# Strassen block products in the last down-projection of a transformer block

## The chip, the cores and the metric

The kernel runs on one core of a Trainium2 chip. The core has engines that run side by side: TensorE multiplies matrices (the profile calls it PE, and its weight loads PEld), VectorE (DVE), ScalarE (ACT) and GpSimd (POOL) work element by element, and SyncE (SP) issues the DMAs. The metric is the device time of one execution in microseconds (us), as a median of several runs.

## The reference

```python
h = x + attention(layernorm(x), wq, wk, wv, wo, beta)     # 2048 tokens, 1024 wide
...
y = layernorm(h)
gate = y @ w1                  # w1, w3: 1024 x 3584
up = y @ w3
out = (silu(gate) * up) @ w2   # w2: 3584 x 1024, the down-projection
return h + out                 # 2048 x 1024, bfloat16
```

The attention works on four segments of 512 tokens with a memory carried between them. It comes first and the change does not touch it.

## The kernel before

The feed-forward part is split into two blocks of 1024 tokens. For each block, `hm[0]` to `hm[27]` hold silu(gate) * up transposed: 128 of the 3584 features on the partitions, the 1024 tokens along the row. `w2` holds all of the 3584 x 1024 weight on the chip, as 28 chunks of 128 rows.

The stages from the end of the attention on are these. `ffn_up(0, ch)` is the up-projection of the first block, in plain matmuls. `ffn_down(0, ...)` is its down-projection. `products7` is the up-projection of the second block, in 28 blocks of 28 matmuls, one for each `hm[n]`; it already takes 2x2 block products with 7 in place of 8 products, with fp16 sums of both operands: `T` holds sums of w1 and w3 columns (VectorE, three instructions a block, L1578), `S` sums of the tokens' tiles, and the products are put together by VectorE in `uu`, `ww` (L1603) and `cc` (L1613) and by GpSimd in `c22` (L1607, the profile calls it c). ScalarE copies partial products out of PSUM (L1600) and takes the silu (L1620, L734). `ffn_down(1, ...)` is the last stage, the down-projection of the second block.

`ffn_down` walks over eight tiles of 128 tokens. For each tile and each half of the 1024 output columns, a group of 28 matmuls (128 tokens x 128 features by 128 features x 512 columns) adds up in one PSUM bank; the groups take turns in banks 2, 3, 4 and 5. VectorE then multiplies by a scale and adds the tile's row of h (`hr`, three buffers, fetched by DMA from `h_scr`), writing `ob` (four buffers), and a DMA stores `ob`. The very last tile has its columns cut into 512, 256, 128 and 128, so that little is left after the last matmul. All matmuls are issued on one line, L763.

`weight_scale` finds power-of-two scales for w1 and w3 from sums of squares: ScalarE squares the weight tiles (L1407), VectorE reduces, one small matmul with a tile of ones adds over the partitions, and VectorE and GpSimd finish the scale. ScalarE multiplies the w1 and w3 tiles by it in `products7` (L734).

Every instruction of these last stages carries a plan time (`G.clock`, in us from the start of `ffn_down(0)`; `MM` = 0.2165 is the planned time of one matmul). Each engine, SP's DMA queue too, issues its instructions strictly in the order of the plan times, and each waits on semaphores for what it reads, and for what still reads or writes what it overwrites. In plan time `products7` begins at 97.0 and `ffn_down(1)` at 266.7. The first small matmul of `weight_scale` has the plan time 55.

Of the kernel before, what the change touches and what calls it, by code (L numbers as in the profile page):

```python
# [17 lines left out]
MM = 0.2165  # L18
# [577 lines left out]
class Kernel:  # L596
# [13 lines left out]
    def plan(self):  # L610
        g = self.g
        at = [16512]
# [49 lines left out]
        r6 = at[0]  # L662
# [17 lines left out]
        last = self.g.base[self.et[8].name][1]  # L680
# [10 lines left out]
        for i, off in enumerate((r2, r2 + 8192)):  # L691
# [28 lines left out]
        self.sq = buf("sq", [128, 32], F32, small + 256)  # L720
        self.sqb = buf("sqb", [128, 2], BF16, small + 384)
        self.sc = buf("sc", [128, 8], F32, small + 416)
# [681 lines left out]
    def squares(self, src, n, early=0):  # L1404

        out, to = self.sq[:, n:n + 1], self.junk2[early]
        return self.g.op("act", act_ns(2048) + 190, lambda e, gr: [e.activation(  # L1407
            to, src, AF.Square, accum_out=out)], reads=[src], writes=[to, out])

# [43 lines left out]
        gr.banks = banks  # L1453
        return gr

    def ffn_down(self, blk, at, inv=None):
        G = self.g
        for i in range(8):
# [5 lines left out]
            cols = [(0, 512), (512, 256), (768, 128), (896, 128)] if t == 15 else [(0, 512), (512, 512)]  # L1464
            for c0, n in cols:
                G.clock = start + 2 * 28 * MM * c0 / 1024
                gr = self.fixed((2, 3, 4, 5)[self.n_ob % 4])
                self.mms(gr, [(lambda gr, n=n: self.bank(gr, 0, n),
                               self.hm[fc][:, i * 128:(i + 1) * 128],
                               self.w2[fc // 4][:, fc % 4, c0:c0 + n],  # L1470
                               fc == 0, fc == 27, n) for fc in range(28)], 8, eager=True,
                         pause=None if t else at + 17.15 + c0 / 10240)
                ob = self.ob[self.n_ob % 4][:, 0:n]
                self.n_ob += 1
                hs = hr[:, c0:c0 + n]
                G.clock = start + 2 * 28 * MM * (c0 + n) / 1024 + (0.3 if t else 13.0)
                if inv is None:
                    G.op("dve", dve_ns(n), lambda e, gr, hs=hs, ob=ob, n=n: [e.tensor_tensor(
                        ob, hs, self.bank(gr, 0, n), op=ALU.add)], reads=[hs], writes=[ob], cls=1,
                        group=gr)  # L1480
                else:
                    G.op("dve", dve_ns(n), lambda e, gr, hs=hs, ob=ob, n=n: [
                        e.scalar_tensor_tensor(ob, self.bank(gr, 0, n), inv, hs, op0=ALU.mult,  # L1483
                                               op1=ALU.add)],
                        reads=[hs, inv], writes=[ob], cls=1, group=gr)
                G.clock += 0.8
                G.dma(self.out2d[t * 128:(t + 1) * 128, c0:c0 + n], ob, cls=1)
# [10 lines left out]
    def weight_scale(self, at):  # L1498

        G = self.g  # L1500
        one, sq, sqb, sc = self.ones[:, :], self.sq, self.sqb[:, :], self.sc
# [9 lines left out]
        G.clock = at + 42.0  # L1511
        n2, al, inv, tmp = (sc[:, 2 * i:2 * i + 2] for i in range(4))
        self.dve_op(lambda e: e.tensor_reduce(n2, sq[:, 0:28].rearrange(
            "p (c b) -> p b c", b=2), mybir.AxisListType.X, ALU.add), 200.0,
                    [sq[:, 0:28]], [n2])
        G.clock += 0.3
        self.dve_op(lambda e: e.tensor_copy(sqb, n2), 200.0, [n2], [sqb])
        G.clock = at + 55.0
# [3 lines left out]
        G.op("dve", 200.0, lambda e, gr: [e.tensor_scalar(n2, self.bank(gr, 0, 2), 1e-30, None,
                                                          op0=ALU.max)], writes=[n2], group=gr)
        G.clock += 0.5
        mh = self.mhalf[:, :].to_broadcast([128, 2])
        self.pool_op(lambda e: e.tensor_tensor(tmp, n2, mh, op=ALU.pow), 1, [n2, self.mhalf[:, :]], [tmp])
        G.clock += 1.0
        ti = tmp.bitcast(I32)
        self.dve_op(lambda e: e.tensor_single_scalar(ti, ti, 0x7F800000, op=ALU.bitwise_and), 200.0,
                    [tmp], [tmp])  # L1530
        G.clock += 0.2
        self.dve_op(lambda e: e.tensor_scalar(al, tmp, 4096.0, None, op0=ALU.mult), 200.0,  # L1532
                    [tmp], [al])
        G.clock += 0.2
        self.dve_op(lambda e: e.reciprocal(inv, al), 200.0, [al], [inv])
        return al, inv

    def token_sums(self, at):
# [9 lines left out]
            self.dve_op(lambda e, o=o, x=x, y=y, op=op: e.tensor_tensor(o, x, y, op=op),  # L1548
                        dve_ns(2048, 2), [x, y], [o])

    def products7(self, at, al, inv):

        G = self.g
        a, b = self.hnT[2], self.hnT[3]
# [2 lines left out]
        for n in range(28):  # L1557
# [39 lines left out]
            u, w, cc = self.uu[:, :], self.ww[:, :], self.cc  # L1597
            for gr, gr2, o, when in ((gb, gc, w, 1.1), (ga, gd, u, 2.85)):
                G.clock = t + when
                G.op("act", act_ns(512), lambda e, gr, o=o: [e.activation(  # L1600
                    o, self.bank(gr), AF.Copy)], writes=[o], group=gr)
                G.clock += 0.85
                G.op("dve", dve_ns(512), lambda e, gr, o=o: [e.tensor_tensor(  # L1603
                    o, self.bank(gr), o, op=ALU.add)], reads=[o], writes=[o], group=gr2)
            c22 = self.c22[:, :]
            G.clock = t + 4.4
            self.pool_op(lambda e: e.tensor_tensor(c22, u, w, op=ALU.add), 512, [u, w], [c22],  # L1607
# [5 lines left out]
            G.op("dve", dve_ns(1024), lambda e, gr, k=k: [e.tensor_tensor(  # L1613
                cc[:, :, :], self.ps[:, (k + 2) * 512:(k + 4) * 512].rearrange(
                    "p (a n) -> p a n", a=2),
                u.unsqueeze(1).to_broadcast([128, 2, 512]), op=ALU.add)],
                reads=[u], writes=[cc[:, :, :]], group=Both(gb, gc))
            g1, g2 = self.gate[:, 0, :], self.gate[:, 1, :]
            G.clock = t + 28 * MM + 0.2
            G.op("act", act_ns(512, 1), lambda e, gr: [e.activation(  # L1620
                g1, self.bank(gr), AF.Silu, scale=inv1)], reads=[inv], writes=[g1], group=ga)
            G.clock = t + 28 * MM + 1.7
            self.act(g2, cc[:, 0, :], AF.Silu, act_ns(512, 1), scale=inv1, extra=[inv])
            for i, (x, y) in enumerate(((g1, cc[:, 1, :]), (g2, c22))):
                G.clock = t + 28 * MM + (1.0, 2.6)[i]
                dst = self.hm[n][:, 512 * i:512 * i + 512]
                self.dve_op(lambda e, dst=dst, x=x, y=y: e.tensor_tensor(dst, x, y, op=ALU.mult),
                            dve_ns(512, 2), [x, y], [dst])

    def tail(self):  # L1630

        self.down_weights()
        self.g.first_planned = len(self.g.ops)
        down = 8 * 56 * MM
        al, inv = self.weight_scale(0.0)
        self.token_sums(50.0)
        self.ffn_down(0, 0.0)
        self.products7(down, al, inv)
        self.ffn_down(1, down + 28 * 28 * MM, inv[:, 0:1])
        self.g.clock = None  # L1640

    def run(self):
# [81 lines left out]
```

## Time and profile before

| | |
|---|---|
| median of 3 runs | 861.01 us (859.96 to 861.49) |
| the profiled execution | 860.11 us, of which the span in the profile is 858.4 us |
| TensorE busy | 853.1 us (99%) |
| VectorE, ScalarE, GpSimd busy | 499.3, 446.6, 209.9 us |
| `products7` | from 589.76 to 758.97 us of the span |
| `ffn_down(1)` | from 758.97 us to the end |
| granted TensorE clock | 1.00 throughout |

Times in the profile count from the start of the span. A row of the timeline gives the start, the duration, the engine, the line of the kernel, the operation, what it writes and reads, and in brackets how long the engine had been idle and what ended the wait. A row of the groups gives the count, the total and the mean of one in ns, and the idle time ahead of them. Matmuls are pipelined: rows that follow one another overlap by 0.16 us, so the pace is read from the starts.

### The profile page before, as it was taken

The page shows a single profiled execution, that of the slowest core. Times are in us where ns is not written, and L with a number is a line of the kernel's source. Part 1 is how long each engine was busy: PE and PEld are TensorE (multiplying, and loading weights), DVE is VectorE, ACT ScalarE, POOL GpSimd, SP SyncE. Part 2 cuts the span into 40 slices and gives each one's busy share as a digit, 9 for nine tenths or more (in the row PEclk, how much of TensorE's full clock was granted, in tenths as well). Part 3 has the DMA queues.
Part 4 walks back from the last instruction along what each step waited for, and adds up shares of the span by engine and source line. Part 5 has one row for each costly group of instructions (what it writes and reads, how often), then busy time and mean ns, then how long its engine had stood idle before and what let it go on. Part 6 is the DMA issues. An engine that isn't in the chain of part 4 may idle for free.

```text
span 858.4 us, 13993 instructions
## 1 busy us (share of the span) xinstructions
PE 853.1 (99%) x5714; PEld 387.2 (45%) x5714; DVE 499.3 (58%) x857; ACT 446.6 (52%) x486; POOL 209.9 (24%) x256
## 2 busy tenths in 40 slices
PE   8999999999999999999999999999999999999998
PEld 5444444444444444444444444444444444444445
DVE  5787887886757677856545511314777777731111
ACT  4878676678746565723432239403777777610000
POOL 1535344326244252501201000000222323210000
DMA  7989957735891718367737199100332234001110
GB/s 233 203 204 215 243 108 208 174 111 160 205 226 51 177 45 204 92 204 189 219 101 196 27 237 300 50 31 18 99 99 82 65 99 123 1 20 50 33 47 25
DMA packets 159664, 111.02 MB, mean 129 GB/s; under 512 B 46832, under 2 KB 145392, under 8 KB 158576
## 3 DMA queue, kind: packets, MB, share of 16 engines
q1 hardware_dynamic: 159600, 110.13, 49.6%
q8 instruction: 45, 0.74, 0.4%
q14 instruction: 19, 0.16, 0.1%
HBM read 90.19 MB, written 9.44 MB: 116 GB/s over the span
## 4 chain that ended last, share of the span: by engine, by line
PE 99%; DMA 1%; SPq 0%; issue 0%; DVE 0%; DVEq 0%
PE ps L763 92%; PE ps L1135 3%; PE ps L1228 3%; DMA wp<-in_A_wk_dram 1%; PE ps L1056 0%; PE ps L1352 0%; SPq L407 0%; PE ps L1221 0%; PE ps L775 0%; DVE ob L1483 0%; DVEq L554 0%
## 5 line engine op out<-in xcount | busy, mean ns | idle before, releaser
L763 PE MATMUL ps<-w2b,hm 128*128 128x512 bf16 (+2 forms) x952 | 194.2, 366 | 0.1
L1149 ACT ACTIVATE et<-ps 128x2048 bf16<-128x2048 f32 x80 | 150.1, 1876 | 47.7 <-PE ps L1135 45.8
L763 PEld LDWEIGHTS ps<-w2b,hm 128*128 128x128 bf16 x952 | 90.7, 98 | 103.2 <-issue 0.5
L1158 POOL TENSOR_SCALAR_AFFINE_SELECT et<-et 128x512 bf16<-128x512 bf16 (+1 forms) x96 | 83.0, 876 | 112.0 <-ACT et L1149 112.0
L763 PE MATMUL ps<-hnT,w1b 128*128 128x512 bf16 x448 | 108.1, 379 | 0.0
L763 PE MATMUL ps<-hnT,w3b 128*128 128x512 bf16 x448 | 107.8, 379 | 0.0
L1607 POOL TENSOR_TENSOR c<-uu,ww 128x512 bf16<-128x512 f32 x28 | 45.7, 1632 | 162.6 <-DVE uu L1603 162.6
L1434 ACT ACTIVATE sg<-ps 128x512 bf16<-128x512 f32 x56 | 33.4, 596 | 97.0 <-PE ps L763 95.8
L763 PE MATMUL ps<-S,T 128*128 128x512 f16 x336 | 81.7, 379 | 0.0
L1437 DVE SCALAR_TENSOR_TENSOR t<-sg,ps 128x512 bf16<-128x512 bf16 x56 | 38.1, 684 | 64.7 <-ACT sg L1434 64.6
L763 PEld LDWEIGHTS ps<-hnT,w1b 128*128 128x128 bf16 x448 | 42.6, 98 | 52.5 <-issue 3.7
L763 PEld LDWEIGHTS ps<-hnT,w3b 128*128 128x128 bf16 x448 | 42.6, 98 | 52.4 <-issue 3.1
L763 PE MATMUL ps<-xnT,wp 128*128 128x512 bf16 (+1 forms) x352 | 60.9, 321 | 1.0 <-DMA wp<-in_A_wk_dram 1.0
L763 PE MATMUL ps<-wo,oT 128*128 128x512 bf16 x256 | 61.1, 380 | 0.0
L734 ACT ACTIVATE wide<-wide,sc 128x2048 bf16<-128x2048 bf16 x28 | 55.6, 1994 | 10.1 <-DVE sc L1532 10.1
L1483 DVE SCALAR_TENSOR_TENSOR ob<-ps,sc,hr 128x512 bf16<-128x512 f32 (+2 forms) x18 | 12.4, 691 | 83.0 <-PE ps L763 83.0
L763 PE MATMUL ps<-hnT,wp 128*128 128x512 bf16 x256 | 59.7, 380 | 0.0
L763 PE MATMUL ps<-hnT,wide 128*128 128x512 bf16 x224 | 57.5, 379 | 0.0
L763 PEld LDWEIGHTS ps<-S,T 128*128 128x128 f16 x336 | 32.9, 98 | 39.6
L1442 DVE SCALAR_TENSOR_TENSOR hm<-t,ps 128x512 bf16<-128x512 bf16 x56 | 37.9, 682 | 19.0 <-PE ps L763 18.3
L1174 DVE TENSOR_TENSOR sum<-sum,et 128x512 bf16<-128x512 bf16 (+1 forms) x64 | 40.6, 642 | 6.1 <-POOL et L1158 3.8
L1613 DVE TENSOR_TENSOR cc<-ps,uu 128x1024 bf16<-128x1024 f32 x28 | 34.3, 1224 | 12.7 <-PE ps L763 12.7
(145 smaller groups left out, 1083.3 us busy)
## 6 DMA issues: line engine op xcount, KB each, us to landing
wide<-in_B_w_dram SPq DMA_DIRECT2D x19, 512.0 KB, 4.1
wide<-in_B_w_dram SPq DMA_DIRECT2D x38, 256.0 KB, 4.6
wp<-in_A_wv_dram SPq DMA_DIRECT2D x8, 1024.0 KB, 5.8
wp<-in_A_wq_dram SPq DMA_DIRECT2D x7, 1024.0 KB, 5.5
wp<-in_A_wk_dram SPq DMA_DIRECT2D x7, 1024.0 KB, 8.0
w1b<-in_B_w_dram SPq DMA_DIRECT2D x14, 512.0 KB, 4.7
w3b<-in_B_w_dram SPq DMA_DIRECT2D x14, 512.0 KB, 4.8
w2b<-in_B_w_dram SPq DMA_DIRECT2D x7, 1024.0 KB, 5.8
```

The source lines that it names most:

```text
L734: return self.g.op("act", cost, lambda e, gr: [e.activation(out, in_, func, scale=scale)], reads=reads, writes=[out], cls=cls, **kw)
L763: return [e.matmul(p[0](gr), p[1], p[2], start=p[3], stop=p[4], **kw) for p in part]
L1135: ins.append(e.matmul(self.bank(gr, j, 512 - 128 * kc, off), k[r, g0 + g, 128 * kc:128 * kc + 128], q[r, g0 + g, 128 * kc:512], start=True ...
L1149: return [e.activation(et[:, :, :], src, AF.Exp, scale=self.scale)]
L1158: self.pool_op(lambda e, v=v, pat=pat: e.affine_select(v, v, pattern=pat, compare_op=ALU.is_ge, fill=0.0, base=0, channel_multiplier=-1), ...
L1174: lambda e, gr: [e.tensor_tensor(o, a, b, op=ALU.add) for o, a, b in sums],
L1228: ins.append(e.matmul(self.ps[32 * i:32 * i + 32, b * 512 + c0:b * 512 + c0 + n], lhsT(i, kc, j), rhs(i, j), start=kc == 0 and j == first, ...
L1434: self.g.op("act", act_ns(512), lambda e, gr, sg=sg: [e.activation(sg, self.bank(gr), AF.Tanh, scale=0.5)], writes=[sg], cls=0, group=gg)
L1437: e.scalar_tensor_tensor(t1, sg, 1.0, self.bank(gr), op0=ALU.add, op1=ALU.mult)], reads=[sg], writes=[t1], cls=0,
L1442: e.scalar_tensor_tensor(dst, t1, 0.5, self.bank(gr), op0=ALU.mult, op1=ALU.mult)], reads=[t1], writes=[dst], cls=0,
L1607: self.pool_op(lambda e: e.tensor_tensor(c22, u, w, op=ALU.add), 512, [u, w], [c22], inputs=2)
L1613: G.op("dve", dve_ns(1024), lambda e, gr, k=k: [e.tensor_tensor(cc[:, :, :], self.ps[:, (k + 2) * 512:(k + 4) * 512].rearrange("p (a n) -> ...
```

## The change

The last stage becomes `down7`. The first two of its eight tiles go through `ffn_down` as before. The other six are taken as three pairs, a and b. A pair's 256 tokens x 3584 features are a 2x2 matrix of blocks (tile a or b, features 0 to 1791 or 1792 to 3583), and w2 is one too (the same halves of the features, columns 0 to 511 or 512 to 1023: b11, b12, b21, b22). In place of eight products of 14 matmuls there are seven: four sums of hm blocks (`Sd`, by VectorE for each pair) and four sums of w2 blocks (`Td`, by VectorE once, the third written over b12) are the operands, all in fp16. Two products continue in a bank that was read halfway. VectorE, ScalarE and GpSimd put the results together with the rows of h, in part by way of three new fp32 tiles `qq`. The pairs use banks 0 to 3 and 4 to 7 in turn.

For the fp16 range w2 gets a power-of-two scale as well: ScalarE squares all of w2 in 14 instructions planned at 44 to 71, the chain of the scale is written as a function, `power`, and runs a second time with its small matmul at 84 (in bank 4), and GpSimd multiplies one chunk of w2 in place in each of the 28 blocks of `products7`. The factor `ka`, which keeps hm in range, goes into five instructions of each block: two copies on ScalarE get a scale, and three additions on VectorE become multiply-adds.

```diff
@@ weight_scale
+        ka, s2, m, m2 = (sc[4][:, 0:1], sc[4][:, 1:2], sc[5][:, 0:1], sc[5][:, 1:2])
...
+        for i in range(14):
+            G.clock = at + 44.0 + 2.1 * i
+            self.squares(self.w2a[:, 2 * i:2 * i + 2, :], 28 + i)
+        be, ib = self.power(28, 1, at + 76.0, at + 84.0, *(t[:, 0:1] for t in sc[6:10]))
@@ products7, in each of the 28 blocks
-                G.op("act", act_ns(512), lambda e, gr, o=o: [e.activation(
-                    o, self.bank(gr), AF.Copy)], writes=[o], group=gr)
+                G.op("act", act_ns(512, 1), lambda e, gr, o=o: [e.activation(
+                    o, self.bank(gr), AF.Copy, scale=ka)], reads=[ka], writes=[o], group=gr)
                 G.clock += 0.85
-                G.op("dve", dve_ns(512), lambda e, gr, o=o: [e.tensor_tensor(
-                    o, self.bank(gr), o, op=ALU.add)], reads=[o], writes=[o], group=gr2)
+                G.op("dve", dve_ns(512), lambda e, gr, o=o: [e.scalar_tensor_tensor(
+                    o, self.bank(gr), ka, o, op0=ALU.mult, op1=ALU.add)], reads=[o, ka],
+                    writes=[o], group=gr2)
+            G.clock = t + 3.1
+            w2 = self.w2[n // 4][:, n % 4, :]
+            self.pool_op(lambda e, w2=w2: e.tensor_scalar(w2, w2, be, None, op0=ALU.mult), 1024,
+                         [w2, be], [w2])
...
+    def down7(self, at, inv):
...
+        self.ffn_down(1, at, inv, 2)
+        for out, x, y, op, when in ((t1, b12, b11, ALU.subtract, 3.4),
+                                    (t2, b22, t1, ALU.subtract, 7.4),
+                                    (t4, b21, t2, ALU.subtract, 11.4),
+                                    (t3, b22, b12, ALU.subtract, 24.4)):
+            for h in range(2):
+                G.clock = at + when + 2.0 * h
+                o, u, v = (z[:, 7 * h:7 * h + 7, :] for z in (out, x, y))
+                self.dve_op(lambda e, o=o, u=u, v=v, op=op: e.tensor_tensor(o, u, v, op=op),
+                            dve_ns(3584, 2), [u, v], [o])
...
+        L = 14 * MM
+        for p in range(1, 4):
+            t = at + 112 * MM + 98 * MM * (p - 1)
+            if p == 1:
+                self.pair_sums(p, [at + 15.5 + 1.4 * i for i in range(4)])
+            else:
+                self.pair_sums(p, [t - 98 * MM + L * i + 0.4 for i in (1, 3, 4, 5)])
+            ha, hb = (self.hr[(8 + 2 * p + i) % 3] for i in range(2))
...
+                G.dma(hr[:, :], self.hd[tile * 128:tile * 128 + 128, :], cls=3)
...
+            product(gc, 0, S[0], t1, True, False)
+            copy(gc, ww, L + 0.3)
+            product(ga, 1, half(0, 0), b11, True, p == 3)
+            copy(ga, u, 2 * L + 0.3)
+            if p == 3:
+                keep(q2, None, ha[:, 0:512], 2 * L + 0.4, ga)
+            product(gd, 2, S[1], t2, True, True)
+            add(gd, u, 3 * L + 0.3)
+            keep(q0, u, ha[:, 512:1024], 3 * L + 1.1)
+            keep(q1, u, hb[:, 0:512], 3 * L + 1.9)
+            product(gb, 3, S[2], t3, True, False)
+            add(gb, ww, 4 * L + 0.3)
+            G.clock = t + 4 * L + 1.1
+            self.pool_op(lambda e: e.tensor_tensor(ww, u, ww, op=ALU.add), 512, [u, ww], [ww],
+                         inputs=2)
+            product(gc, 4, S[3], b22, False, True)
+            give(None, q0, 0, 512, 5 * L + 0.3, gc)
+            give(ww, hb[:, 512:1024], 1, 512, 5 * L + 1.2)
+            product(gb, 5, half(1, 1), t4, False, True)
+            give(None, q1, 1, 0, 6 * L + 0.3, gb)
+            if p < 3:
+                product(ga, 6, half(0, 1), b21, False, True)
+                give(None, ha[:, 0:512], 0, 0, 7 * L + 0.3, ga)
+                continue
+            for i, (c0, n) in enumerate(((0, 256), (256, 128), (384, 128))):
+                gr = self.fixed(4 + i)
+                product(gr, 6, half(0, 1), b21, True, True, c0, n, L * c0 / 512)
+                give(None, q2[:, c0:c0 + n], 0, c0, 6 * L + L * (c0 + n) / 512 + 0.3, gr, n)
@@ tail
-        self.ffn_down(1, down + 28 * 28 * MM, inv[:, 0:1])
+        self.down7(down + 28 * 28 * MM, inv2)
```

Here `product` issues 14 matmuls, the second argument being its place in the pair; `copy` is a copy from PSUM by ScalarE; `add` and `keep` are VectorE instructions of 512 elements; `give` is the VectorE instruction that writes `ob`, with the DMA that stores it.

More of the change, by code (lines that the diff above doesn't have):

```diff
@@ L719, in plan @@
         self.ones = buf("ones", [128, 128], BF16, small)
-        self.sq = buf("sq", [128, 32], F32, small + 256)
-        self.sqb = buf("sqb", [128, 2], BF16, small + 384)
-        self.sc = buf("sc", [128, 8], F32, small + 416)
+        self.sq = buf("sq", [128, 48], F32, small + 256)
+        self.sqb = buf("sqb", [128, 2], BF16, small + 448)
+        self.sc = buf("sc", [128, 24], F32, small + 480)
         ring = base[self.h[0].name][1] - 2048
@@ L727, in plan @@
                   for i in range(4)]
+        hn0 = base[self.hnT[0].name][1]
+        t1, t2, t4 = (buf(f"Td{i}", [128, 14, 512], F16, hn0 + 14336 * i)[:, :, :]
+                      for i in range(3))
+        t3 = self.w2a[:, :, :].bitcast(F16)[:, 0:14, 512:1024]
+        self.Td = (t1, t2, t3, t4)
+        self.Sd = [buf(f"Sd{i}", [128, 14, 128], F16, p) for i, p in enumerate(
+            (wo + 10240, wo + 13824, wo + 17408, hn0 + 43008))]
+        self.qq = [buf(f"qq{i}", [128, 512], F32, base[self.wide[2].name][1] + 2048 * i)
+                   for i in range(3)]
         self.hd = g.dram("h_scr", [2048, 1024], BF16)
@@ L1454, in fixed, with ffn_down @@
         return gr
-    def ffn_down(self, blk, at, inv=None):
+    def ffn_down(self, blk, at, inv=None, tiles=8):
         G = self.g
-        for i in range(8):
+        for i in range(tiles):
             t = 8 * blk + i
@@ L1500, in weight_scale @@
         G = self.g
-        one, sq, sqb, sc = self.ones[:, :], self.sq, self.sqb[:, :], self.sc
+        one, sc = self.ones[:, :], self.sc
         G.clock = at + 1.0
@@ L1510, in weight_scale @@
                 self.squares(self.wide[slot][:, 8 * b:8 * b + 8, :], 2 * ch + b)
[L1511 to L1518, printed above, removed]
+        sc = [sc[:, 2 * i:2 * i + 2] for i in range(12)]
@@ new lines, in weight_scale, with tiny, power @@
+        for i in range(14):
+            G.clock = at + 44.0 + 2.1 * i
+            self.squares(self.w2a[:, 2 * i:2 * i + 2, :], 28 + i)
+        be, ib = self.power(28, 1, at + 76.0, at + 84.0, *(t[:, 0:1] for t in sc[6:10]))
+        self.tiny(lambda e: e.tensor_tensor(m2, m, ib, op=ALU.mult), sc[5], m2, ib)
+        return al, inv, ka, s2, be, m2
+    def tiny(self, f, src, out, *more):
+        self.g.clock += 0.2
+        self.dve_op(f, 200.0, [src, *more], [out])
+    def power(self, c0, k, when, then, n2, al, inv, tmp):
+        G = self.g
+        sq, sqb = self.sq[:, c0:c0 + (28 if k == 2 else 14)], self.sqb[:, 0:k]
+        G.clock = when
+        self.dve_op(lambda e: e.tensor_reduce(n2, sq.rearrange("p (c b) -> p b c", b=k),
+                                              mybir.AxisListType.X, ALU.add), 200.0, [sq], [n2])
+        self.tiny(lambda e: e.tensor_copy(sqb, n2), n2, sqb)
+        G.clock = then
@@ L1519, in weight_scale @@
         gr = self.fixed(4)
-        self.mms(gr, [(lambda gr: self.bank(gr, 0, 2), one, sqb, True, True, 2)], 8)
-        G.clock = at + 56.0
-        G.op("dve", 200.0, lambda e, gr: [e.tensor_scalar(n2, self.bank(gr, 0, 2), 1e-30, None,
+        self.mms(gr, [(lambda gr: self.bank(gr, 0, k), self.ones[:, :], sqb, True, True, k)], 8)
+        G.clock += 1.0
+        G.op("dve", 200.0, lambda e, gr: [e.tensor_scalar(n2, self.bank(gr, 0, k), 1e-30, None,
                                                           op0=ALU.max)], writes=[n2], group=gr)
@@ L1628, in products7, with pair_sums, half @@
                             dve_ns(512, 2), [x, y], [dst])
+    def pair_sums(self, p, when):
+        G = self.g
+        def half(i, k):
+            c = slice(i * 128, i * 128 + 128)
+            return [self.hmA[:, 14 * k:25 if k else 14, c]] + [self.hmB[:, :, c]] * k
+        a, b = 2 * p, 2 * p + 1
+        s1, s2, s3, s4 = (t[:, :, :] for t in self.Sd)
+        for out, x, y, op, t in ((s1, half(b, 0), half(b, 1), ALU.add, when[0]),
+                                 (s2, [s1], half(a, 0), ALU.subtract, when[1]),
+                                 (s3, half(a, 0), half(b, 0), ALU.subtract, when[2]),
+                                 (s4, half(a, 1), [s2], ALU.subtract, when[3])):
+            G.clock = t
+            cut = [(0, 11), (11, 14)] if len(x) + len(y) > 2 else [(0, 14)]
+            for i, (lo, hi) in enumerate(cut):
+                o, u, v = (z[i] if len(z) > i else z[0][:, lo:hi, :] for z in ([out[:, lo:hi, :]] * 2, x, y))
+                if len(cut) > 1:
+                    u, v = (z[:, lo:hi, :] if z.shape[1] == 14 and i == 0 else z for z in (u, v))
+                self.dve_op(lambda e, o=o, u=u, v=v, op=op: e.tensor_tensor(o, u, v, op=op),
+                            dve_ns(128 * (hi - lo), 2), [u, v], [o])
```

99 lines of the change are left out of this document (78 added, 21 removed).

## The prediction

> **What bounds the kernel now.** I read the page first, then the chain that ended last, then busy time by stage, and at last the timeline of the two stages that the change touches.
>
> ```profile
> span 858.4 us, 13993 instructions
> PE 853.1 (99%) x5714; PEld 387.2 (45%) x5714; DVE 499.3 (58%) x857; ACT 446.6 (52%) x486; POOL 209.9 (24%) x256
> ...
> PE 99%; DMA 1%; SPq 0%; issue 0%; DVE 0%; DVEq 0%
> ```
>
> The chain is TensorE from end to end, so a matmul taken out shortens the kernel if nothing makes TensorE wait in its place. The next view has two stages as windows, the seven-product up-projection (589.76 to 758.97) and the last down-projection behind it.
>
> ```profile
> core 0: us, PE busy (x) PEld busy (x) DVE busy (x) ACT busy (x) POOL busy (x), PEclk, DMA share, GB/s
> ...
> 589.76:758.97 169.21, 169.21 (x786) 76.71 (x784) 128.16 (x222) 116.59 (x136) 45.70 (x28) 1.00 0.26 73
> 758.97:858.40 99.43, 97.00 (x505) 46.94 (x503) 13.92 (x21) 1.30 (x2) 0.00 (x0) 1.00 0.12 38
> ```
>
> TensorE never pauses in either; VectorE is busy 76% of the first and 14% of the second. The clock is 1.00. The last down-projection in order of time (start, duration, engine, line):
>
> ```profile
> 752.92 1.89 PE L763 MATMUL ps<-S,T 128*128 128x512 f16 x8
> ...
> 758.97 16.35 PE L763 MATMUL ps<-w2b,hm 128*128 128x512 bf16 x75
> ...
> 765.29 0.75 DVE L1483 SCALAR_TENSOR_TENSOR ob<-ps,sc,hr 128x512 bf16<-128x512 f32 x1 [4.29 <-PE ps L763]
> ...
> 849.92 0.75 DVE L1483 SCALAR_TENSOR_TENSOR ob<-ps,sc,hr 128x512 bf16<-128x512 f32 x1 [5.32 <-PE ps L763]
> 852.95 0.48 DVE L1483 SCALAR_TENSOR_TENSOR ob<-ps,sc,hr 128x256 bf16<-128x256 f32 x1 [2.28 <-PE ps L763]
> 854.51 0.35 DVE L1483 SCALAR_TENSOR_TENSOR ob<-ps,sc,hr 128x128 bf16<-128x128 f32 x1 [1.08 <-PE ps L763]
> 856.07 0.35 DVE L1483 SCALAR_TENSOR_TENSOR ob<-ps,sc,hr 128x128 bf16<-128x128 f32 x1 [1.21 <-PE ps L763]
> ```
>
> Each row of VectorE follows a finished group of 28 matmuls. From 765.29 to 849.92 lie 14 groups of 512 columns: 84.63 / 392 = 0.2159 us a matmul. The 256-column group took 3.03 us (0.108 each), each 128-column one 1.56 (0.0557 each). Products of mixed bf16 and fp16 run as fast: the 28 of one block from 752.92 to 758.97 take 6.05, or 0.2161 each.
>
> **The change part by part.**
>
> *Matmuls.* Before, the stage has 420 matmuls of 512 columns, 28 of 256 and 56 of 128: 90.68 + 3.03 + 3.12 = 96.8 us. After, the first two tiles keep 112; each pair needs 7 products of 14 instead of 8, so the pairs issue 280 of 512 columns, and the last product of the last pair is cut into 14 of 256 and 28 of 128. That is 392 x 0.2159 + 1.51 + 1.56 = 87.7 us. Gain 9.1 us. The end stays as it was: a 128-column evacuation and one small store.
>
> *Sums on VectorE in the first 24.2 us of the stage.* New are four sums of w2 in eight pieces of 3584 elements and four sums of hm for the first pair. The nearest rows are sums of 16-bit operands:
>
> ```profile
> 542.27 1.22 DVE L1548 TENSOR_TENSOR S<-hnT 128x2048 f16<-128x2048 bf16 x1
> ...
> 751.21 0.68 DVE L1578 TENSOR_TENSOR T<-wide 128x1024 f16<-128x1024 bf16 x1
> ```
>
> Their slope is 0.54 / 1024 = 0.527 ns an element over 0.14 us fixed: a piece takes 2.03 us, an hm sum 1.09 in one piece or 1.24 in two. In issue order, counted from 758.97: VectorE is free at about 2.0 (last hm product), T1 done at 6.1, first evacuation 7.1, T2 11.1, T4 and the second evacuation 16.0, S1 17.2, S2 18.3, S3 19.4, third evacuation 20.2, S4 21.4. T3 overwrites a quarter of w2, which tile 9 has read at 21.2, and is done at 27.3 after the fourth evacuation. TensorE wants T1 and S1 at 24.2, T2 and S2 at 30.2, T3 and S3 at 33.3. The least margin is 6 us, so I cost these at nothing; the cover is the two tiles left in their plain form. At half that rate (1.05 ns an element, as the 0.69 us addition ww of 512 elements from PSUM, further down, has it) S1 would come at some 31 and T3 at 45. That is the upper end, below under rivals.
>
> *Inside a pair.* VectorE gets per pair 4.7 us of sums for the next pair, two additions of 0.69, two new multiply-adds into qq and four outputs of 0.75 (row at 765.29): 10.5 of 21.2 us. The tightest wait is product 5, which continues a bank that VectorE must first have read for product 3: queued ahead of that read are one addition, S2 and two multiply-adds, 3.5 us from the end of product 2 on, so the read ends 1.2 us into product 4's 3.02 us. Margin 1.8 us.
>
> *The DMA queue.* The second tile row of h for pairs 2 and 3 waits for a buffer that the pair before reads until its last output, and SP holds the output stores behind it for about 13 us.
>
> ```profile
> hr<-h_scr SPq DMA_DIRECT2D x16, 256.0 KB, 3.2
> out_dram<-ob SPq DMA_DIRECT2D x31, 128.0 KB, 1.7
> ```
>
> The row of h is issued 0.8 us after that output and lands 3.2 us later, while its first reader comes some 11 us into the pair; the four outputs held up have four buffers, and the next output is due 15 us on. Nothing.
>
> *The scale of w2.* Fourteen squares of 2048 elements join ScalarE, and a second small matmul with its chain.
>
> ```profile
> 538.71 1.91 ACT L1407 ACTIVATE junk<-wide 128x2048 bf16<-128x2048 bf16 x1
> 540.53 0.19 ACT L1407 ACTIVATION_READ_ACCUMULATOR junk<-wide 128x1 f32 x1
> 550.81 5.79 ACT L734 ACTIVATE wide<-wide,sc 128x2048 bf16<-128x2048 bf16 x3 [10.10 <-DVE sc L1532]
> ...
> 548.29 0.17 PE L763 MATMUL ps<-sqb,ones 128*128 128x2 bf16 x1
> 548.32 41.60 PE L763 MATMUL ps<-w2b,hm 128*128 128x512 bf16 x192
> ...
> 548.52 0.16 DVE L1522 TENSOR_SCALAR sc<-ps 128x2 f32<-128x2 f32 x1
> ...
> 584.62 0.68 DVE L1578 TENSOR_TENSOR T<-wide 128x1024 f16<-128x1024 bf16 x1
> ```
>
> At 2.1 us each they run from 540.7 to 570.2; the three scalings move to 570.3 to 576.1, and 584.62 wants two of them. The small matmul is placed at plan time 84, that is 13.0 us ahead of 589.76, at 576.8: its sum is ready at 570.7, margin 6 us. It costs 0.03 us of TensorE (548.29 to 548.32). The group that takes its bank next starts four matmuls (0.86 us) later and needs VectorE's read, which by the rows ended 0.39 us after the matmul's start: no wait, at most 0.1 us.
>
> *The up-projection.* Three VectorE steps in each of the 28 blocks become multiply-adds with a pointer scalar (0.75, the outputs at 765.29, against 0.69, ww below), so 0.18 us a block; two ScalarE copies get a pointer scale, which costs 0.09 (0.69 against 0.60 below) on an engine busy 69% of this stage. New is one GpSimd multiplication of 1024 bf16 elements in place, queued right behind the addition c of the block before.
>
> ```profile
> 751.38 1.64 POOL L1607 TENSOR_TENSOR c<-uu,ww 128x512 bf16<-128x512 f32 x1 [4.40 <-DVE uu L1603]
> 752.33 1.23 DVE L1613 TENSOR_TENSOR cc<-ps,uu 128x1024 bf16<-128x1024 f32 x1 [0.44 <-PE ps L763]
> 753.21 0.69 ACT L1620 ACTIVATE gate<-ps,sc 128x512 bf16<-128x512 f32 x1 [2.94 <-PE ps L763]
> 753.47 0.41 DVE L1578 TENSOR_TENSOR T<-T,wide 128x512 f16<-128x512 f16 x1
> 753.93 0.42 DVE L1627 TENSOR_TENSOR hm<-gate,cc 128x512 bf16<-128x512 bf16 x1
> 753.99 0.60 ACT L1600 ACTIVATE ww<-ps 128x512 f32<-128x512 f32 x1
> 754.27 0.42 DVE L1578 TENSOR_TENSOR T<-wide,T 128x512 f16<-128x512 bf16 x1
> 754.92 0.69 DVE L1603 TENSOR_TENSOR ww<-ps,ww 128x512 f32<-128x512 f32 x1 [0.24 <-PE ps L763]
> 755.51 1.03 PE L763 MATMUL ps<-S,T 128*128 128x512 f16 x4
> 756.65 0.69 DVE L1603 TENSOR_TENSOR uu<-ps,uu 128x512 f32<-128x512 f32 x1 [0.70 <-PE ps L763]
> 757.42 1.26 POOL L1607 TENSOR_TENSOR c<-uu,ww 128x512 bf16<-128x512 f32 x1 [4.40 <-DVE uu L1603]
> ...
> L1607 POOL TENSOR_TENSOR c<-uu,ww 128x512 bf16<-128x512 f32 x28 | 45.7, 1632 | 162.6 <-DVE uu L1603 162.6
> L1158 POOL TENSOR_SCALAR_AFFINE_SELECT et<-et 128x1024 bf16<-128x1024 bf16 x32 | 39.3, 1230 | 50.9 <-ACT et L1149 50.8
> ...
> L1578 DVE TENSOR_TENSOR T<-wide x27: 678/681/682, 594.1 to 751.2; 128x1024 f16<-128x1024 bf16 x27
> ...
> L1174 DVE TENSOR_TENSOR sum<-et,et x32: 636/684/1409, 24.3 to 363.2; 128x1024 bf16<-128x1024 bf16 x32
> ```
>
> The price of the GpSimd step is not in the trace. Nearest is the affine select of 1024 bf16 in place with one input, 1.23 us; the upper end is c's 1.63 for 512 elements doubled, about 3.1, the lower end nothing. I take 1.23. Alone, c takes 1.26; beside T's sum, which started 0.17 us earlier, 1.64, while that sum stays at 0.68 in all 27 cases. Where GpSimd's selects run in the attention, a sum of two SBUF tiles reaches 1.41 against a median of 0.68. So one of the two engines waits, and here GpSimd would start first: c ends at 753.02, the new step holds until about 754.25, and VectorE's sum due at 753.47 slips by 0.8 us. TensorE wants its result at 755.51 and would have it at 754.7. Behind it VectorE's queue has 0.24 us of idle time ahead of ww and 0.70 ahead of uu, which take the 0.8 up before the next block. So it costs nothing at 1.23 us.
> The Trainium skill, "SBUF — State Buffer", section "Who interferes with whom", says that a VectorE instruction with two SBUF inputs and a GpSimd one that reads SBUF exclude each other, the first to issue holding the shared ports for its whole length. The 1.41 agrees with it; by proportional sharing instead the sum would slip less, and by either the stage would keep its time.
>
> **Sum.** 9.1 us less, and up to 0.2 for small waits that I take as nothing. The profiled execution took 860.11 us with its span of 858.4, so it would take 851.0, span 849.3. The median of the runs is 861.01, 0.90 above that execution: 861.0 - 9.1 = 851.9.
>
> **Rivals.**
> *The new GpSimd step makes VectorE late* (ends slower). Place: the 28 blocks. The sum due at 753.47 has to end about 0.1 us ahead of 755.51 and takes 0.42, so GpSimd may hold the ports until 755.0, a step of 2.0 us; beyond that every block loses the excess. The gain is used up at 9.1 / 28 = 0.33 us, a step of 2.3. At 3.1 us it is 28 x 1.1 = 31 us, 883. For it speaks 1.63 for c; against it that c has two fp32 inputs, and the one-input select costs 1.2 ns an element. Chance 5%, with 872 for a step of 2.7.
> *The first pair waits for its sums.* If the new operands, in rows 1024 elements apart, lose the rate of the 0.68 us row, S1 comes 7 us late and T3 another 5: 12 us, 864. Against it: T's operands are strided too. A milder lateness in the pairs gives 853 to 860. Chance 3% for the first, 8% for the second.
> *TensorE waits for the scale of w2.* Each us by which the squares end after 576 is a us lost; 29 us of squares would have to take over 35. Some 856, chance 2%.
> *Fewer matmuls take as long,* because products of two fp16 operands or of strided hm columns run slower: 861. The 0.2161 of the mixed block speaks against it. Chance 2%.
>
> **How the numbers follow.** My forecast, 851.9, has 80%, with its own range from 850.9 (runs differ by about 1 us) to 853.0. With the milder lateness the range reaches 854.5, and holds some 83%. No change that can be told from the measurement is within 0.2%, 1.7 us. Faster by more: 80 + 8 + 2 = 90%; slower: 5 + 3 = 8%; the rest 2%.
>
> **What the profile after would show.** TensorE at 99%, no idle time in the window of the last stage, and that stage some 9.1 us shorter; the w2 multiplication at about 1.2 us, with T's 512-element sums starting 0.8 us later and TensorE's rows 6.05 us a block as now; squares of w2 ending near 570; S1 ready about 7 us ahead of the first pair. Waits of TensorE on VectorE at line 763 would prove me wrong: in the 28 blocks through GpSimd, at the first pair through the sums.

## The result and the profile after

The changed kernel takes 851.82 us in the median of four runs (851.17 to 852.06), the kernel before 860.66 in those runs: a ratio of 0.9896, 95% interval 0.9879 to 0.9913. A second set of runs on one chip (`after_again` below) has 851.82 against 860.91, 0.990 (0.9883 to 0.9918). The forecast was 851.9. Part of that closeness is luck: the two medians differ by 8.84 us and not by 9.1, and the kernel before came out 0.35 below the 861.01 from which the forecast starts.

The page of the changed kernel, its head and the chain that ended last:

```profile
span 850.2 us, 13983 instructions
PE 845.0 (99%) x5645; PEld 381.7 (45%) x5645; DVE 551.0 (65%) x906; ACT 483.3 (57%) x520; POOL 295.0 (35%) x288
PE 99%; DMA 1%; SPq 0%; issue 0%; DVE 0%; DVEq 0%
```

Busy time in its last two stages, in the columns of the same view of before:

```profile
590.67:759.89 169.22, 169.22 (x785) 76.70 (x784) 142.19 (x222) 121.79 (x136) 121.78 (x55) 1.00 0.26 73
759.89:850.20 90.31, 87.87 (x435) 41.30 (x433) 50.45 (x60) 4.88 (x8) 5.35 (x3) 1.00 0.14 41
```

The last stage went from 99.43 to 90.31 us, 9.12 less. The up-projection ahead of it takes 169.22 where it took 169.21, though VectorE is busy 14 us more in it and GpSimd 76 us more. The two profiled executions differ by only 8.2 us in their spans, because the last stage begins 0.92 later after the change. Most of that lies at the very beginning, where nothing was changed. A row of the chain that ended last, of before and of after:

```profile
3.14 5.70 DMA wp<-in_A_wk_dram
```

```profile
3.12 6.41 DMA wp<-in_A_wk_dram
```

The first weights landed 0.7 us later in the second. Such differences between executions are what the medians even out.

The first pair of the last stage in order of time, after the change:

```profile
759.89 5.56 PE L776 MATMUL ps<-w2a,hmA 128*128 128x512 bf16 x25
...
776.07 0.35 DVE L1686 TENSOR_TENSOR Sd<-hmA,hmB 128x384 f16<-128x384 bf16 x1
...
784.07 3.18 PE L776 MATMUL ps<-Td,Sd 128*128 128x512 f16 x14
...
784.94 2.02 DVE L1704 TENSOR_TENSOR w2a<-w2a 128x3584 f16<-128x3584 bf16 x1
...
793.13 6.21 PE L776 MATMUL ps<-w2a,Sd 128*128 128x512 f16 x28
```

S1 ends at 776.42, 16.5 us into the stage, and its product begins at 784.07 without a wait. T3, written over a quarter of w2, ends at 786.96, 27.1 into the stage, for a product that starts 33.2 into it.

One row of the groups holds the surprise. The multiplication of w2 by GpSimd, priced at 1.23 us, takes 2.85:

```profile
L1639 POOL TENSOR_SCALAR w2a<-w2a,sc 128x1024 bf16<-128x1024 bf16 x28 | 79.7, 2848 | 7.0 <-PE ps L776 7.0
```

By the prediction's own bounds a step over 2.0 us would hold VectorE too long, and every block would lose the excess: 28 x 0.85 = 24 us. Nothing was lost. The durations of VectorE's sum (min/median/max in ns) and the timeline of one block show why:

```profile
L1609 DVE TENSOR_TENSOR T<-T,wide x28: 419/921/1219, 591.6 to 754.5; 128x512 f16<-128x512 f16 x28
```

```profile
741.91 2.83 POOL L1639 TENSOR_SCALAR w2a<-w2a,sc 128x1024 bf16<-128x1024 bf16 x1
742.37 0.92 DVE L1609 TENSOR_TENSOR T<-T,wide 128x512 f16<-128x512 f16 x1
743.22 0.41 DVE L1663 TENSOR_TENSOR hmA<-gate,cc 128x512 bf16<-128x512 bf16 x1
743.55 0.41 DVE L1609 TENSOR_TENSOR T<-wide,T 128x512 f16<-128x512 bf16 x1
```

The sum is held up: it takes 0.92 us where it took 0.415 before. So it was free to run at 742.88, 0.97 us after GpSimd began. The two instructions behind it run at their own 0.41, though GpSimd is at work until 744.74. GpSimd keeps VectorE waiting for the first third of this instruction, not for all of it. The experiments ask what sets these 0.97 us, and whether the rest of the change is as free as it looks.

### The profile page after: what moved, and what is told of

Same layout as the page of the kernel before. It is cut to its first block, busy times and chain, and to the rows that moved or that the text cites. A ratio compares the mean times of both kernels' runs of the same rounds, so it can differ in the third digit from the quotient of the medians.

```text
span 850.2 us, 13983 instructions
## 1 busy us (share of the span) xinstructions
PE 845.0 (99%) x5645; PEld 381.7 (45%) x5645; DVE 551.0 (65%) x906; ACT 483.3 (57%) x520; POOL 295.0 (35%) x288
## 4 chain that ended last, share of the span: by engine, by line
PE 99%; DMA 1%; SPq 0%; issue 0%; DVE 0%; DVEq 0%
PE ps L776 92%; PE ps L1148 3%; PE ps L1241 3%; DMA wp<-in_A_wk_dram 1%; PE ps L1069 0%; PE ps L1365 0%; SPq L407 0%; PE ps L1234 0%; PE ps L788 0%; DVE ob L1752 0%; DVEq L554 0%
## 5 line engine op out<-in xcount | busy, mean ns | idle before, releaser
L776 PE MATMUL ps<-w2a,hmA 128*128 128x512 bf16 (+2 forms) x597 | 129.1, 371 | 0.1
L776 PEld LDWEIGHTS ps<-w2a,hmA 128*128 128x128 bf16 x597 | 57.5, 98 | 67.1 <-issue 0.5
L1639 POOL TENSOR_SCALAR w2a<-w2a,sc 128x1024 bf16<-128x1024 bf16 x28 | 79.7, 2848 | 7.0 <-PE ps L776 7.0
L1456 DVE SCALAR_TENSOR_TENSOR hmA<-t,ps 128x512 bf16<-128x512 bf16 x50 | 34.0, 683 | 18.8 <-PE ps L776 18.5
L1649 DVE SCALAR_TENSOR_TENSOR cc<-ps,sc,uu 128x1024 bf16<-128x1024 f32 x28 | 35.9, 1284 | 11.2 <-PE ps L776 11.2
```

Source lines behind the costliest of these rows:

```text
L776: return [e.matmul(p[0](gr), p[1], p[2], start=p[3], stop=p[4], **kw) for p in part]
L1456: e.scalar_tensor_tensor(dst, t1, 0.5, self.bank(gr), op0=ALU.mult, op1=ALU.mult)], reads=[t1], writes=[dst], cls=0,
L1639: self.pool_op(lambda e, w2=w2: e.tensor_scalar(w2, w2, be, None, op0=ALU.mult), 1024, [w2, be], [w2])
L1649: G.op("dve", dve_ns(1024), lambda e, gr, k=k: [e.scalar_tensor_tensor(cc[:, :, :], self.ps[:, (k + 2) * 512:(k + 4) * 512].rearrange("p ( ...
```

## The experiments

My theory: the gain is the 42 matmuls alone; all added work lies beside TensorE's matmuls; the two plain tiles are what hides VectorE's sums; and GpSimd's step is free because it holds VectorE only in its first part. The rivals: the added work costs a little in each block; the sums were never in need of cover; the hold is that of the whole instruction, or a fixed time.

**The scale of w2 taken away** (`no_scale`).

```diff
-        for i in range(14):
-            self.squares(self.w2a[:, 2 * i:2 * i + 2, :], 28 + i)
-        be, ib = self.power(28, 1, at + 76.0, at + 84.0, ...)
...
-            self.pool_op(lambda e, w2=w2: e.tensor_scalar(w2, w2, be, None, op0=ALU.mult), 1024, ...)
```

> The changed kernel without the scale of w2: no squares of w2, no second chain and small matmul, no GpSimd multiplication in the 28 blocks; w2 goes into the fp16 sums as it is. Theory (all of this work lies beside TensorE's matmuls): the time of the changed kernel, 851.8 us, to within 0.1%; the sum T<-T,wide falls back from 0.92 to 0.42 us, and the 28 blocks take 169.2 us as before. Rival (GpSimd's hold on VectorE or the squares cost TensorE a little in each block): 0.1 us a block or more, so 849 us or less.

851.91 us (851.0 to 852.6), ratio to before 0.9891 (0.9878 to 0.9905), the changed kernel's 0.9896. The sum is back at its own pace:

```profile
L1604 DVE TENSOR_TENSOR T<-T,wide x28: 414/415/418, 591.2 to 754.1; 128x512 f16<-128x512 f16 x28
```

So 80 us of GpSimd's work, 29 of ScalarE's, and half a microsecond of hold in each block cost nothing that can be measured.

**The last stage back to plain matmuls, all else kept** (`plain_down`).

```diff
-        self.down7(down + 28 * 28 * MM, inv2)
+        self.ffn_down(1, down + 28 * 28 * MM, inv2)     # eight tiles, the last cut as before
```

> The changed kernel with its scale of w2, the GpSimd multiplications and the factor ka, but the last down-projection of all eight tiles in plain matmuls as before, so 42 matmuls more. Theory (the gain is the 42 matmuls of 0.216 us alone, and what was added ahead of the last stage costs nothing): the time of the kernel before, 860.7 us, ratio 1.000. Rival (something else of the change gives or takes time): off from it by over 1.5 us.

860.48 us against 860.84, ratio 0.9992 (0.9983 to 1.0001). The whole gain is in the stage with fewer matmuls.

**Half the cover** (`one_tile`).

```diff
-        self.ffn_down(1, at, inv, 2)
+        self.ffn_down(1, at, inv, 1)                    # T3 moved up behind S4, pairs 12.1 us earlier
```

> The changed kernel with one plain tile ahead of the three pairs in place of two; tile 9 of the second block is left out (its rows of the output are not written). The cover of VectorE's sums falls from 24.2 to 12.1 us. Theory (S1 is the sum that the first pair waits for; it ends 16.5 us into the stage whatever the cover): 851.8 - 12.1 + 4.5 = 844.2 us, with one idle stretch of TensorE of 4 to 5 us at the first product of the first pair. Rival (the sums are not what the two plain tiles cover): 839.7 us and no idle stretch.

845.52 us (845.1 to 846.6). The timeline at the first product of the first pair:

```profile
776.10 0.35 DVE L1686 TENSOR_TENSOR Sd<-hmA,hmB 128x384 f16<-128x384 bf16 x1
776.24 4.59 PE L776 MATMUL ps<-Td,Sd 128*128 128x512 f16 x14 [4.07 <-DVE Sd L1686]
...
777.07 0.15 PEld L776 LDWEIGHTS ps<-Td,Sd 128*128 128x128 f16 x1 [0.28 <-issue]
777.50 0.15 PEld L776 LDWEIGHTS ps<-Td,Sd 128*128 128x128 f16 x1 [0.28 <-issue]
...
780.67 3.19 PE L776 MATMUL ps<-w2a,hmA 128*128 128x512 bf16 x14
```

TensorE waits 4.07 us for S1, which ends 16.5 us into the stage as it does with two tiles. That is the theory's wait, in its place. The time is 1.3 above the forecast for another reason: the 14 matmuls behind the wait take 4.43 us, from start to start, in place of 3.02. Their weight loads, one for each matmul, come 0.43 us apart until 779.16, twice the usual 0.216, so TensorE ran at half its pace for 2.9 us. Busy time in two windows, with the granted clock as the third column from the end:

```profile
755.00:775.00 20.00, 17.07 (x78) 7.60 (x78) 17.59 (x17) 3.22 (x5) 3.13 (x2) 1.00 0.03 2
775.00:790.00 15.00, 13.71 (x57) 5.99 (x59) 12.67 (x16) 1.20 (x2) 0.00 (x0) 0.89 0.18 51
```

The clock of 0.89 over those 15 us is a deficit of 1.6, near the 1.41 lost. The Trainium skill, "TensorE: Matmul & The Clock Gate", section "What's actually happening", says that TensorE's clock falls to half after some 3.4 us without work, until it has been busy about as long again. The 4.07 us here and the 2.9 us at half pace behind them agree with it roughly, and the waits of 1.9 us and less in the runs below (`all4`, `pool_2048`, granted clock 1.00) showed no such loss.

**GpSimd with more work than a block has time for, and with just less** (`extra_1024`, `extra_512`).

```diff
             self.pool_op(lambda e, w2=w2: e.tensor_scalar(w2, w2, be, None, op0=ALU.mult), 1024, ...)
...
+            self.pool_op(lambda e, w2=w2, jk=jk: e.tensor_scalar(jk, w2, be, None, op0=ALU.mult), 1024, ...)
```

(The other kernel has 512 in the added line.)

> The changed kernel with a second GpSimd multiplication of 1024 elements in each of the 28 blocks (the same operands, the product goes to a tile that nobody reads). GpSimd then has 2.84 + 2.84 + 1.64 = 7.3 us of work in a block of 6.04. Theory (GpSimd has 1.58 us to spare in a block, and beyond that the addition c, and through the tile uu the copies out of PSUM, become late): GpSimd sets the pace, 28 x 1.27 = 36 us more, about 887. Rival (GpSimd's lateness does not reach TensorE, whose products do not read c): 852.

> The changed kernel with a second GpSimd multiplication in each of the 28 blocks, of 512 elements (the product goes to a tile that nobody reads), some 1.45 us by the 2.84 of 1024. GpSimd then has 5.9 us of work in a block of 6.04. Theory (GpSimd's 1.58 us of idle time in a block is all that may be added): no longer than 852.5. Rival (GpSimd's work costs in proportion before its idle time is used up, 30.5 us for 1024 elements): about 867.

With 1024 elements 882.38 us (882.1 to 882.6), with 512 851.44 (850.9 to 852.4). A stretch of the first in order of time, and two rows of its waits (total, times, longest):

```profile
692.52 1.04 PE L776 MATMUL ps<-hnT,T 128*128 128x512 bf16 x4 [1.07 <-ACT ww L1631]
...
697.72 1.26 POOL L1648 TENSOR_TENSOR c<-uu,ww 128x512 bf16<-128x512 f32 x1
...
699.08 0.69 ACT L1631 ACTIVATE ww<-ps,sc 128x512 f32<-128x512 f32 x1 [2.95 <-POOL c L1648]
...
699.82 1.04 PE L776 MATMUL ps<-hnT,T 128*128 128x512 bf16 x4 [1.08 <-ACT ww L1631]
```

```profile
ACT ww L1631 <- POOL c L1648: 73.5, 26, 3.2
...
PE ps L776 <- ACT ww L1631: 26.5, 25, 1.3
```

A block now takes 7.30 us (692.52 to 699.82), GpSimd's own work: 2.84, 3.15 and, for c, 1.26 us. The expected 2.84 + 2.84 + 1.64 comes to the same sum by other parts. The chain is the one expected but for the tile: ScalarE's copy into ww waits until c has read it, and TensorE waits for that copy. There are 25 such waits and not 28, since the first blocks still live on GpSimd's slack: 30.6 us more, 36 expected. With 512 elements GpSimd has 2.84 + 1.56 + 1.60 = 6.00 us in a block of 6.04, and nothing is lost. GpSimd's idle time can be filled almost to its end for nothing; beyond it every tenth of a microsecond counts in each block.

**The hold: fewer and longer steps, more and shorter ones** (`pool_2048`, `pool_512`), with trials of single instructions (`probe`, `probe2`).

```diff
-            w2 = self.w2[n // 4][:, n % 4, :]
+            w2 = self.w2a[:, n - n % 2:n - n % 2 + 2, :]      # only where n is even; 2048 elements
...
+            for hh in range(2):                               # pool_512: two steps a block
+                w2 = self.w2[n // 4][:, n % 4, 512 * hh:512 * hh + 512]
```

> The changed kernel with w2 multiplied by GpSimd in 14 steps of 2048 elements, one in every second block, in place of 28 of 1024. Theory (GpSimd keeps VectorE's sum of two SBUF tiles waiting only while it reads its input, 0.97 us for 1024 elements, 1.85 for 2048): in every second block T<-T,wide takes up to 1.8 us, in the others 0.42; the time stays 851.8, since TensorE asks for the result 2.5 us into the block. Rival 1 (a fixed hold of 0.97 us for any instruction): 0.92 us as now, same time. Rival 2 (the hold lasts as long as the instruction, some 5.5 us): 28 / 2 x 3 = 42 us more.

> The changed kernel with six trials in the first down-projection, where VectorE is mostly idle: a GpSimd instruction on a scratch tile, and about 0.1 us after its start a VectorE instruction on another tile (a subtraction of two SBUF tiles of 512 bf16, 0.42 us when alone; in the last trial a copy of 1024 bf16). GpSimd's instructions in order: multiply by a pointer scalar, 1024; by an immediate, 1024; by a pointer scalar, 512; the same, 2048; memset of 1024; by a pointer scalar, 1024, against the copy. Theory (hold while GpSimd reads): VectorE's subtraction takes 1.3 us, 1.3 or less, 0.8, 2.2, and 0.42 beside the memset. Rival (fixed hold): 1.3 in all that read. On the price: if the pointer makes the multiplication dear, the immediate one takes about 1.2 us as the affine select, else 2.8. On the copy: if it needs the ports for the whole of GpSimd's instruction it takes about 3 us, if only for its reading about 1.2. The kernel's time: the small chain of the scale may be delayed, 852 to 855.

`pool_2048` takes 872.52 us (872.2 to 873.6): 20.7 more than the changed kernel. One of its even blocks, and VectorE's sum over all blocks:

```profile
670.75 5.43 POOL L1640 TENSOR_SCALAR w2a<-w2a,sc 128x2048 bf16<-128x2048 bf16 x1
671.21 3.52 DVE L1609 TENSOR_TENSOR T<-T,wide 128x512 f16<-128x512 f16 x1
...
674.79 0.39 PE L776 MATMUL ps<-S,T 128*128 128x512 f16 x1 [1.43 <-DVE T L1609]
```

My theory of 1.85 us fell here, and both rivals with it: the sum could run 3.56 us after GpSimd's start, not after 0.97, 1.85 or 5.43. TensorE waits 1.43, and thirteen such waits make 18.9 us, nearly all of the loss:

```profile
PE ps L776 <- DVE T L1609: 18.9, 13, 1.7
```

This is what the prediction had feared, with nearly the right bound: it put the longest hold that costs nothing at 2.0 us, and 3.56 less the wait of 1.43 is 2.1.

The trials show the same by themselves; the two kernels that hold them take 851.52 and 852.04 us, in one execution each. The rows are GpSimd's instruction, and VectorE's subtraction of 512 elements (0.42 us alone; in the last row a copy of 1024). From `probe`:

```profile
557.32 2.87 POOL L1543 TENSOR_SCALAR px<-px,sc 128x1024 bf16<-128x1024 bf16 x1
557.44 1.27 DVE L1554 TENSOR_TENSOR px<-px 128x512 bf16<-128x512 bf16 x1 [0.26 <-POOL px L1549]
...
560.27 2.78 POOL L1543 TENSOR_SCALAR px<-px 128x1024 bf16<-128x1024 bf16 x1
...
565.07 5.44 POOL L1543 TENSOR_SCALAR px<-px,sc 128x2048 bf16<-128x2048 bf16 x1
...
566.95 2.11 DVE L1554 TENSOR_TENSOR px<-px 128x512 bf16<-128x512 bf16 x1
...
573.57 2.85 POOL L1543 TENSOR_SCALAR px<-px,sc 128x1024 bf16<-128x1024 bf16 x1
573.70 1.26 DVE L1558 COPY px<-px 128x1024 bf16<-128x1024 bf16 x1 [0.26 <-POOL px L1549]
```

The hold of 1024 elements is 0.97 us again (557.44 + 1.27 - 0.42 - 557.32). That of 2048 is 3.57 (566.95 + 2.11 - 0.42 - 565.07), though the subtraction came only 1.88 us behind GpSimd's start. The copy beside GpSimd ended at 574.96, long before GpSimd at 576.42; how long it takes alone no run shows. The multiplication by an immediate takes 2.78, so the pointer is not what makes it dear; 2.85 us is its price here too, where VectorE has little to do. Two trials of this set say nothing of the hold. The memset had nothing beside it. With 512 elements the subtraction, 0.05 us behind GpSimd's start, took its own 0.43, and GpSimd took 1.82 in place of 1.56: here it seems to have been GpSimd that waited. So a second set was made, with the subtraction some 0.2 us behind GpSimd's start, and `pool_512` put the rule that I had then to a test.

> The changed kernel with five trials in the first down-projection, VectorE's subtraction (0.42 us alone) issued some 0.2 us behind GpSimd's start: multiplications of 512, 768 and 1536 elements, a memset of 1024, and a product of two bf16 tiles of 512. By a hold until 1.87 us before the end: none for 512, 0.3 us for 768 (end at 2.2), 2.3 us for 1536 (end at 4.15), so the subtraction takes 0.42, 0.5 and 2.5 us; by a hold of a third of the length 0.7, 0.9 and 1.6. Memset: 0.42, since it reads nothing. Two tiles: not known.

> The changed kernel with w2 multiplied by GpSimd in 56 steps of 512 elements, two in each block. Theory (GpSimd keeps VectorE's sum of two SBUF tiles waiting until 1.87 us before its own end, as 2.84 - 0.97 and 5.43 - 3.56 both give; a step of 512 takes 1.56, so it holds nothing): T<-T,wide at 0.42 to 0.5 us in all blocks, time as the changed kernel. Rival (a hold in proportion to the length, a third of it, or a fixed one): 0.5 us or more of hold twice a block, T<-T,wide still at 0.6 us or more; same time.

```profile
555.59 1.59 POOL L1543 TENSOR_SCALAR px<-px,sc 128x512 bf16<-128x512 bf16 x1
555.84 0.72 DVE L1558 TENSOR_TENSOR px<-px 128x512 bf16<-128x512 bf16 x1
...
561.65 4.16 POOL L1543 TENSOR_SCALAR px<-px,sc 128x1536 bf16<-128x1536 bf16 x1
...
561.90 3.30 DVE L1558 TENSOR_TENSOR px<-px 128x512 bf16<-128x512 bf16 x1
...
567.62 0.95 POOL L1545 MEMSET px<- 128x1024 bf16 x1
...
567.92 0.43 DVE L1558 TENSOR_TENSOR px<-px 128x512 bf16<-128x512 bf16 x1
...
573.73 1.15 POOL L1546 TENSOR_TENSOR px<-px 128x512 bf16<-128x512 bf16 x1
...
573.99 1.17 DVE L1558 TENSOR_TENSOR px<-px 128x512 bf16<-128x512 bf16 x1
```

The holds are 0.55 us for 512, 0.76 for 768 (not shown), 0.97 for 1024, 3.13 for 1536 and 3.56 for 2048, and none for the memset, which reads nothing. A product of two tiles of 512 on GpSimd, the trial for which nothing was forecast, held 1.01 of its own 1.15 us. The rule "1.87 us before the end" fell: by it 512 would hold nothing and 1536 2.3 us. What the five have is one slope, 0.42 us for 512 elements, up to 1024 and again from 1536 on, with a step of 1.7 us between. That fits an instruction that reads up to 1024 elements in one go, works them out before it reads the next, and lets VectorE in only when the last are read. The numbers fit this; no run shows the reading itself.

The trace of before had the figure already:

```profile
118.84 1.10 POOL L1158 TENSOR_SCALAR_AFFINE_SELECT et<-et 128x1024 bf16<-128x1024 bf16 x1 [5.28 <-ACT et L1149]
119.08 1.40 DVE L1174 TENSOR_TENSOR sum<-et,et 128x1024 bf16<-128x1024 bf16 x1
```

VectorE's sum, 0.68 us alone, was free to run at 119.80, 0.96 us after GpSimd's start. The select takes 1.10, so there the hold looks like the whole instruction. Beside the slower multiplication the two come apart: with 1024 elements to read GpSimd holds VectorE for 0.96, 0.97 and 1.01 us, in instructions of 1.10, 2.84 and 1.15.

`pool_512` takes 851.52 us (851.2 to 852.7), as expected; its T<-T,wide has a median of 0.49 us and goes up to 0.80, since each short step still holds 0.55 us.

**All four pairs as seven products** (`all4`, `all4b`). The half-cover run says that the two plain tiles are there for 16.5 us of VectorE's sums. They could go if the sums came in the order in which the products want them, and if T1 were ready at the start.

```diff
+            if n % 2:                                  # products7: T1 chunk by chunk over b12
+                self.dve_op(... e.tensor_tensor(o, x, y, op=ALU.subtract) ...)
...
-        self.ffn_down(1, at, inv, 2)
-        for p in range(1, 4):
+        for p in range(4):                             # first pair: products 1, 0, 6, 2, 3, 4, 5
```

> All four pairs of the last down-projection as seven products; no plain tile. T1 is taken chunk by chunk in the up-projection (14 sums of 512 elements by VectorE, one in every second block, over b12 in place), T3 as T2 - b11. In the first pair the order of the products is 1, 0, 6, 2, 3, 4, 5, so that S1, S2, T2, T3, S4 and T4 come one after another as TensorE reaches them; the other pairs begin with 1, 0. Theory (TensorE bounds, and VectorE makes the first pair wait about 0.4 us for S1 and 0.6 us for T4, at the rates of the trace): 14 matmuls fewer, 3.0 us, less 1.0: about 849.8. Rival (VectorE's sums have no cover without the plain tiles, the first pair waits for more than 3 us): 852 or more.

850.73 us (850.0 to 850.9). It gains 1.1 over the changed kernel, not 2.0. The wait for T4 is 1.9 us, where 0.6 was reckoned:

```profile
774.61 5.02 DVE L1717 TENSOR_TENSOR Td<-w2a,Td 128x3584 f16<-128x3584 bf16 x2
...
779.68 1.69 PE L776 MATMUL ps<-Td,hmA 128*128 128x512 f16 x7 [1.91 <-DVE Td L1717]
```

The two halves of T4 take 5.02 us in place of 3.95, beside GpSimd's addition into ww (774.77 to 777.75), and VectorE had been idle for 0.85 us before, waiting for product 3. The next version takes the first half of T4 into that gap, and holds GpSimd's addition back until T4 is done:

```diff
-                                  (t4, b21, t2, 16.3, 18.3)):
+                                  (t4, b21, t2, 15.3, 18.3)):
...
+            if z:
+                G.dep(o, last)                         # the addition waits for T4's second half
```

> The version with four pairs, with the first half of T4 taken between the two additions (VectorE was idle there for 0.85 us) and GpSimd's addition of the first pair held back until T4 is done (beside it T4's second half took 3.0 in place of 2.0 us). Theory (the 1.9 us for which TensorE waited for T4 come from these two): no wait over 0.3 us in the last stage, 3.0 us less than the changed kernel, 848.8. Rival (VectorE has simply too much to do in the first pair): the wait moves to another sum, 850 or more.

> The changed kernel itself, once more, for comparison on one chip: 851.8 us.

849.55 us (849.3 to 849.7) against 851.82 (851.3 to 853.2) for the changed kernel and 860.91 for the one before, on one chip; its ratio to the kernel before is 0.9868 (0.9853 to 0.9884). The profile has no wait of TensorE for a sum in the last stage any more. The two halves of T4 take 2.02 us each; the two changes were made together, so what each is worth alone is not shown:

```profile
774.33 2.02 DVE L1717 TENSOR_TENSOR Td<-w2a,Td 128x3584 f16<-128x3584 bf16 x1
...
776.86 2.02 DVE L1717 TENSOR_TENSOR Td<-w2a,Td 128x3584 f16<-128x3584 bf16 x1
```

The last stage begins here with

```profile
759.90 3.19 PE L776 MATMUL ps<-w2a,hmA 128*128 128x512 bf16 x13
```

and ends with the span of 847.2 us: 87.3 us, 3.0 less than the changed kernel's 90.31, the price of the 14 matmuls. The medians differ by 2.3 and not by the 3.0 that were forecast. In the two profiled executions the stage began 0.3 us later than in `after_again` (759.90 against 759.60), as `products7` did already (590.68 against 590.39), so T1's 14 sums cost that stage nothing, and 0.35 more lay outside the span (849.30 - 847.2 against 851.65 - 849.9); why, the runs do not show. This version beats both.

## Why the prediction was right

*Matmuls.* The term of 9.1 us came out at 9.12 in the stage, and `plain_down` shows that it is the whole gain.

*Sums on VectorE.* S1 was put 17.2 us into the stage and came at 16.5, T3 at 27.3 and came at 27.1. `one_tile` shows that the cover named is the one that counts.

*The DMA queue.* The row of h of the second pair was issued 0.1 us after the end of the last output of the first (0.8 after its start, as reckoned), and the four stores came behind it, with no wait of TensorE or VectorE for them.

*The scale of w2.* The squares ended at 568.99, reckoned at 570.2, and the small matmul ran at 577.71 without a wait. `no_scale` bears out that its price is nothing.

*The up-projection.* The total of nothing is right, its working is not: two errors cancelled, which is luck. The step was sized at 1.23 us by the affine select and took 2.85, near the upper end of 3.1. And a step was held to keep VectorE waiting for all its length, by which 2.85 us would have cost some 24 us and made the kernel slower; it holds for 0.97, and the sum slipped by 0.5 us where 0.8 was forecast. The row behind that rule, the 1.41 us of a sum beside a select, could not tell a hold of 0.96 from the select's whole 1.10. The bound on the hold itself, 2.0 us, is what `pool_2048` bears out: 3.56 us of hold made TensorE wait 1.43. So the rival in which GpSimd makes VectorE late had 5% on a wrong footing: the price it needed was there, and only the length of the hold kept it away.

## What to carry to other kernels

Where TensorE is the bound and never idle, matmuls taken out come off the time one for one, as long as each operand made elsewhere is ready when its product is due: work the margins out in the order in which the making engine issues, and put the products that need nothing first. For an engine that must not be kept waiting, ask for how long the other engine keeps it waiting, not how long its instruction runs. A GpSimd multiplication like this one is better issued in steps of at most 1024 elements. An operation that the trace of before lacks is not priced by a row that merely looks alike; the range should then take its upper end seriously.

## What the hardware showed that was not expected

- A GpSimd multiplication of bf16 elements by a scalar costs 1.56 us for 512, 2.84 for 1024 and 5.43 for 2048, some 2.5 ns for each element more. An immediate in place of the pointer changes little (2.78 for 1024). The affine select of 1024 takes 1.23 in the mean, and 1.10 where nothing holds it up.
- That multiplication keeps a VectorE sum of two SBUF tiles waiting for 0.55, 0.97, 3.13 and 3.56 us with 512, 1024, 1536 and 2048 elements. The Trainium skill, "SBUF — State Buffer", section "Who interferes with whom", has the hold last for the whole instruction; these runs do not agree, and the measurement decides. What goes with the hold is the number of elements read: 1024 hold for 0.96 us in a select of 1.10, for 0.97 in a multiplication of 2.84, and for 1.01 in a product of two tiles that takes 1.15. A memset on GpSimd, which reads nothing, held up nothing (0.43 us beside it), as that section says.
- After 4.07 us without work TensorE's next 14 matmuls took 1.41 us longer than their 3.02: they came 0.43 us apart for 2.9 us, then 0.216.
